# Linear attention and two expert layers: attention rebuilt on strips of the array, half of the weight conversions placed behind it

## The chip, the cores and the metric

The kernel runs on one core of one Trainium2 chip. The metric is device microseconds of one launch; the host's arrangement of arrays before and after the launch is outside it. Before the change three runs gave 2201.4, 2201.72 and 2202.03 us: a median of 2201.72 us.

## The reference

```python
def phi(x):                                     # w_phi: 64 x 128
    proj = einsum('bhsd,df->bhsf', x, w_phi)
    proj = proj - max(abs(proj), axis=-1)
    return concatenate([exp(proj), exp(-proj)])
q_p, k_p = phi(q), phi(k)                       # q, k, v: 4 batches x 8 heads x 576 tokens x 64
kv  = einsum('bhsf,bhsd->bhfd', k_p, v);  z = sum(k_p, axis=2)
x   = (q_p @ kv) / (q_p @ z + 1e-6)             # -> 2304 tokens x 512
h   = x @ w_in;  x = (h * cos(h)) @ w_out       # w_in 512 x 2048, w_out 2048 x 512: 64-bit floats
P   = exp(x @ w_gate - max), 8 rounds of row and column scaling   # 2304 x 8
out = sum over e of P[:, e] * (relu(x @ w1[e]) @ w2[e])           # 8 experts, w1 512 x 1024
```

## The kernel before

Three stages follow each other. **Attention** works on 16 pairs of heads (4 batches x 4 pairs). Of the 576 tokens of a head 512 are "main" and 64 are the "rest"; the rests of two heads fill 128 partitions together. **The first expert layer** goes through blocks 0 to 3 (the main tokens of a batch, 512 columns) and block 4 (all rests, 256 columns, beside block 3) with 16 units of weights, each made of half a unit from `w_in` and half from `w_out`. **The second expert layer** runs over 8 experts x 4 quarters, twice, with a seven-product scheme (`layer1`) and an accumulation (`layer2`).

Products in the expert layers split each operand into a rounded high part (`act_hi`, ScalarE) and the rest (`dve_lo` or `pool_lo`) and add three products (`mm3`). The 64-bit weights of the first layer come as pairs of 32-bit words and are converted on the chip: 32 halves, one for each half unit. For one half (`conversion`, lines 128 to 169) the low word goes through ScalarE (`csgn`), the high word through three VectorE operations (`cmag`: mask, floor with 2^-15, shift) and one that puts sign and low bits together; GpSimd joins them, ScalarE rounds (`csp`), GpSimd makes the rest, and a transfer writes both to device memory (`wd`). `load_unit1` fetches a unit from there (`wsp`, four buffers).

One round of attention works on three pairs at once, each at another stage: the newest pair is loaded, turned (`turn_heads`, transposes of `kraw` and `qraw` into `pa`, split into `Th` and `Tl`) and projected (`project`, a block-diagonal `w_phi` for two heads, three products); the pair before gets its key sums (`key_sums`, `pk`: 2 heads x 2 signs x 5 products, with ones beside `v` for the denominator), its query features (`query_features`, transposes into `pu`) and its quotient (`attend`, `pn`); the oldest is turned back (`emit_x`, `px`). The maximum of the absolute value and the subtraction (`center`, tiles `m` and `u`) are VectorE's, the exponentials (`exps`) ScalarE's. [...]

In attention each engine runs in the written order: while `pinned[0]` is set, every operation is kept in program order. The order of the steps is the string `ORDER`, once a round, 18 rounds in all (line 517). A step `k` resumes the conversion, four times a round, so all 32 halves are through before the first layer begins. Outside attention the planner may bring ready work forward on an engine. In the first layer `moe1_steps` yields four times a unit; for block 0 each second yield resumes whatever is left of the conversion (line 577), and `next_unit` resumes it until the unit asked for is there (line 529). All transfers are issued by SyncE, in one queue.

Of the kernel before, what the change touches and what calls it, by code (L numbers as in the profile page):

```python
# [25 lines left out]
def kernel(ctx: ExitStack, tc: tile.TileContext, q, k, v, w_phi,  # L26
                         moe_w_in, moe_w_out, moe2_w_gate, moe2_w1, moe2_w2, out):
    nc = tc.nc
    B, H, S, D = q.shape
    NT, DM = out.shape  # L30
    DFF = moe_w_out.shape[0]
    NE, _, DF2 = moe2_w1.shape
    P = 128
    NP = H // 2
    KC = DM // P
    NF1 = DFF // P
    NF2 = DF2 // P
    MAIN = 512
    REM = S - MAIN
# [4 lines left out]
    NTT = NT // P  # L44
# [73 lines left out]
    ps_a = actx.enter_context(tc.tile_pool(name="ps_a", bufs=7, space=PSUM, side="right"))  # L118
    turn = [0]

    def apsum(name):
        return ps_a.tile([P, 512], F32, name=name, tag="pa")

    wd = [dpool.tile([P, 2, 2, DM], F32, name=f"wd{f}") for f in range(NF1)]
    win32 = moe_w_in.bitcast(I32)
    wout32 = moe_w_out.bitcast(I32)

    def conversion():
        n = 2 * NF1
        raws, mags, sps = {}, {}, {}  # L130

        def fetch(h):
            f, i = divmod(h, 2)
            raw = vpool.tile([P, DM, 2], I32, name="raw64")
            if i == 0:
                nc.sync.dma_start(out=raw.rearrange("p (k f) t -> p k (f t)", k=KC),
                                  in_=win32[:, f * 2 * P:(f + 1) * 2 * P].rearrange("(k p) f -> p k f", p=P))
            else:
                nc.sync.dma_start(out=raw.rearrange("p f t -> p (f t)"), in_=wout32[f * P:(f + 1) * P, :])
            raws[h] = raw  # L140

        fetch(0)
        yield
        for h in range(n + 1):
            if h > 0:
                sps[h - 1] = vpool.tile([P, 2, DM], F32R, name="csp")
                act_hi(sps[h - 1][:, 0, :], mags[h - 1].bitcast(F32))
            if h < n:
                if h + 1 < n:
                    fetch(h + 1)  # L150
                hw = raws[h][:, :, 1]
                mag = vpool.tile([P, DM], I32, name="cmag", bufs=CB)
                sgn = vpool.tile([P, DM], I32, name="csgn", bufs=CB)
                se.activation(out=sgn.bitcast(F32), in_=raws[h][:, :, 0].bitcast(U32), func=AF.Copy,
                                     scale=2.0 ** -51, bias=2.0)
                ve.tensor_scalar(out=mag, in0=hw, scalar1=2 ** 31 - 1, scalar2=None, op0=ALU.bitwise_and)
                ve.tensor_scalar(out=mag.bitcast(F32), in0=mag.bitcast(F32), scalar1=2.0 ** -15, scalar2=None, op0=ALU.max)
                ve.tensor_scalar(out=mag, in0=mag, scalar1=3, scalar2=None, op0=ALU.logical_shift_left)
                mags[h] = mag
            yield  # L160
            if h < n:
                ve.scalar_tensor_tensor(out=sgn, in0=hw, scalar=-2 ** 31, in1=sgn, op0=ALU.bitwise_and, op1=ALU.bitwise_or)
                ge.tensor_tensor(out=mag, in0=mag, in1=sgn, op=ALU.add)
            if h > 0:
                sp = sps.pop(h - 1)
                pool_lo(sp[:, 1, :], mags.pop(h - 1).bitcast(F32), sp[:, 0, :])
                nc.sync.dma_start(out=wd[(h - 1) // 2][:, (h - 1) % 2, :, :], in_=sp.bitcast(F32))
                done_conv[0] = h // 2
            yield

    vx_t = []
    for i in range(2):
        t = apool.tile([P, 10, P], F32, name=f"vx{i}", bufs=1)
        ge.memset(t, 0.0)
        ge.memset(t[:, 0:8, D:P], 1.0)
        ge.memset(t[0:D, 8, D:P], 1.0)
        ge.memset(t[D:P, 9, D:P], 1.0)
        vx_t.append(t)
# [4 lines left out]
    def load_pair_rest(src, b, p, t):  # L183
        for a in range(2):
            nc.sync.dma_start(out=t[D * a:D * a + D, 8, :], in_=src[b, 2 * p + a, MAIN:S, :])

    def load_pair(src, b, p, nm, part=False):
        t = apool.tile([P, 9, D], F32, name=nm)
        nc.sync.dma_start(
            out=t[:, 0:8, :].rearrange("p (h j) d -> p h (j d)", h=2),  # L190
            in_=src[b, 2 * p:2 * p + 2, 0:MAIN, :].rearrange("h (p j) d -> p h (j d)", j=4))
        if not part:
            load_pair_rest(src, b, p, t)
        return t

    def load_v(b, p):
        t = vx_t[p % 2]
        for a in range(2):
            nc.sync.dma_start(out=t[:, 4 * a:4 * a + 4, 0:D],
                              in_=v[b, 2 * p + a, 0:MAIN, :].rearrange("(p j) d -> p j d", j=4))  # L200
            nc.sync.dma_start(out=t[D * a:D * a + D, 8 + a, 0:D], in_=v[b, 2 * p + a, MAIN:S, :])
        return t

    raw0 = [load_pair(k, 0, 0, "kraw", True)]
    wblk = apool.tile([P, 4, P], F32, name="wblk", tag="u", bufs=4).rearrange("p a f -> p (a f)")[:, 0:2 * P]
    ve.memset(wblk, 0.0)
    nc.sync.dma_start(out=wblk[0:D, 0:P], in_=w_phi)
    nc.sync.dma_start(out=wblk[D:P, P:2 * P], in_=w_phi)
    wblkh = apool.tile([P, 2 * P], F32R, name="wblkh", bufs=1)
    wblkl = apool.tile([P, 2 * P], F32R, name="wblkl", bufs=1)  # L210
    split(wblk, wblkh, wblkl, act_hi, dve_lo)
    wrem = apool.tile([P, P], F32, name="wrem", bufs=1)
    ve.tensor_copy(wrem, wblk[:, P:2 * P])
    load_pair_rest(k, 0, 0, raw0[0])
    raw0.append(load_pair(q, 0, 0, "qraw"))
    GQ = P // KC
    graw = const.tile([P, KC, GQ], F32, name="graw")
    ge.memset(graw, 0.0)
    nc.sync.dma_start(out=graw[:, :, 0:NE], in_=moe2_w_gate.rearrange("(k p) e -> p k e", p=P))
# [15 lines left out]
    def load_heads(b, p):  # L235
        st = {"b": b, "p": p}
        st["raw"] = raw0 if (b, p) == (0, 0) else [load_pair(k, b, p, "kraw"), load_pair(q, b, p, "qraw")]
        st["vx"] = load_v(b, p)
        st["u"], st["kp"], st["qp"], st["T"] = {}, {}, {}, {}
        return st  # L240

    def turn_heads(st, part):
        if part == "r":
            st["Tr"] = apool.tile([P, 2, P], F32, name="Tr", bufs=1)
            pr = apsum("pr")
            for s in range(2):
# [27 lines left out]
    def project_rem(st):  # L274
        pp = apsum("pp")
        for s in range(2):
            pe.matmul(pp[:, s * P:(s + 1) * P], st["Tr"][:, s, :], wrem, start=True, stop=True)
        u = apool.tile([P, 2, P], F32, name="urem", bufs=1)
        center(pp, 2, u)
        st["u"][2] = u[:, 1, :]  # L280
        t = apool.tile([P, 2, P], F32, name="kp1", bufs=1)
        st["kp"][2] = t
        defer(KD, lambda: exps((t[:, 0, :], t[:, 1, :]), u[:, 0, :]))
        yield 0.44

    def project(st, s, unit):
        pp = apsum("pp")
        for w in range(2):
            th, tl = [x[:, 2 * unit + w, :] for x in st["T"][s]]
            mm3(pp[:, 256 * w:256 * w + 256], [((th, tl), (wblkh, wblkl))])  # L290
# [272 lines left out]
    while late:  # L563
        tick()
# [318 lines left out]
```

## Time and profile before

| | before |
|---|---|
| median of three runs | 2201.72 us |
| profiled execution: its own time | 2202.81 us |
| its span, first to last instruction | 2201.0 us |
| mean granted TensorE clock | 0.998 |
| TensorE busy | 2173.4 us (99%), 12871 matmuls |
| VectorE, ScalarE, GpSimd busy | 1311.0, 963.6, 1076.8 us |

The span differs from the execution's own time by what lies around the first and last instruction. Matmuls are pipelined and their ends are modelled: a busy TensorE is one with work under way, not one at its peak. A merged row of the timeline gives the first start and the time to the last end; the spacing of equal instructions is read from it by taking off the length of the last.

### The profile page before, as it was taken

The page shows a single profiled execution, that of the slowest core. Times are in us where ns is not written, and L with a number is a line of the kernel's source. Part 1 is how long each engine was busy: PE and PEld are TensorE (multiplying, and loading weights), DVE is VectorE, ACT ScalarE, POOL GpSimd, SP SyncE. Part 2 cuts the span into 40 slices and gives each one's busy share as a digit, 9 for nine tenths or more (in the row PEclk, how much of TensorE's full clock was granted, in tenths as well). Part 3 has the DMA queues.
Part 4 walks back from the last instruction along what each step waited for, and adds up shares of the span by engine and source line. Part 5 has one row for each costly group of instructions (what it writes and reads, how often), then busy time and mean ns, then how long its engine had stood idle before and what let it go on. Part 6 is the DMA issues. An engine that isn't in the chain of part 4 may idle for free.

```text
span 2201.0 us, 33288 instructions
## 1 busy us (share of the span) xinstructions
PE 2173.4 (99%) x12871; PEld 1940.4 (88%) x12871; DVE 1311.0 (60%) x2492; ACT 963.6 (44%) x1565; POOL 1076.8 (49%) x712
## 2 busy tenths in 40 slices
PE   8999999999999999999999999999999999999999
PEld 8999888887887888988998998998998999999998
DVE  7888744335534876666666655555555555555555
ACT  5666555555553343343343343333433433433431
POOL 2233400000005577577577576576676676676662
PEclk9999999999999999999999999999999999999999
DMA  6766455556433112222222111441111111111101
GB/s 188 242 197 193 141 185 200 195 204 213 139 113 102 39 65 66 86 81 75 77 70 91 60 59 49 139 141 49 40 48 48 46 41 49 49 39 48 49 29 44
DMA packets 143631, 219.57 MB, mean 100 GB/s; under 512 B 36336, under 2 KB 94832, under 8 KB 143472
## 3 DMA queue, kind: packets, MB, share of 16 engines
q1 hardware_dynamic: 143472, 217.44, 30.1%
q8 instruction: 101, 1.65, 0.3%
q14 instruction: 58, 0.48, 0.1%
HBM read 182.93 MB, written 34.47 MB: 99 GB/s over the span
## 4 chain that ended last, share of the span: by engine, by line
PE 84%; DVE 10%; POOL 2%; DMA 1%; issue 1%; SPq 1%; ACT 1%; POOLq 0%; DVEq 0%; ACTq 0%
PE py L70 35%; PE pm L70 31%; PE ph L70 9%; PE acc L70 8%; DVE m L70 2%; DVE u L70 2%; DVE cmag L70 2%; POOL cmag L70 1%; DVE csgn L70 1%; POOL csp L70 1%; DVE rd L70 0%; DVE xn L70 0%; PE pn L70 0%; DMA raw<-in_moe_w_dram 0%; DVE xl L70 0%
## 5 line engine op out<-in xcount | busy, mean ns | idle before, releaser
L787 DVE SCALAR_TENSOR_TENSOR acc<-py,logit,acc 128x512 f32<-128x512 f32 x531 | 396.6, 750 | 322.2 <-PE py L70 322.2
L70 PE MATMUL pm<-xch,w1h 128*128 128x288 f32 x1792 | 531.0, 296 | 3.1 <-DVE t L815 1.3
L70 PE MATMUL pm<-xch,w1l 128*128 128x288 f32 x1792 | 530.6, 297 | 0.0
L70 PE MATMUL pm<-xcl,w1h 128*128 128x288 f32 x1792 | 523.0, 292 | 0.0
L682 POOL TENSOR_TENSOR w1l<-raw,w1h 128x256 fp32r<-128x256 f32 x126 | 97.1, 792 | 824.4 <-ACT w1h L679 824.4
L70 PE MATMUL py<-w2h,hl 128*128 128x512 f32 x1152 | 452.0, 392 | 3.6 <-POOL hl L70 3.6
L70 PE MATMUL py<-w2l,hh 128*128 128x512 f32 x1152 | 451.6, 392 | 0.0
L70 PE MATMUL py<-w2h,hh 128*128 128x512 f32 x1152 | 450.6, 391 | 0.8 <-DVE acc L787 0.8
L70 POOL TENSOR_TENSOR hl<-r,hh 128x1152 fp32r<-128x1152 f32 x128 | 344.7, 2693 | 78.8 <-ACT hh L70 73.0
L70 PEld LDWEIGHTS pm<-xcl,w1h 128*128 128x128 f32 x1792 | 341.1, 190 | 5.3 <-issue 0.4
L70 PEld LDWEIGHTS pm<-xch,w1h 128*128 128x128 f32 x1792 | 336.6, 188 | 9.7 <-DVE t L815 1.6
L70 PEld LDWEIGHTS pm<-xch,w1l 128*128 128x128 f32 x1792 | 336.1, 188 | 0.0
L761 ACT ACTIVATE r<-r 128x1152 f32<-128x1152 f32 x128 | 149.1, 1165 | 268.4 <-DVE r L741 262.1
L70 PEld LDWEIGHTS py<-w2h,hl 128*128 128x128 f32 x1152 | 216.9, 188 | 50.1 <-POOL hl L70 4.3
L70 PEld LDWEIGHTS py<-w2h,hh 128*128 128x128 f32 x1152 | 217.0, 188 | 44.9 <-DVE acc L787 2.8
L70 PEld LDWEIGHTS py<-w2l,hh 128*128 128x128 f32 x1152 | 216.9, 188 | 42.5
L737 ACT COPY keep<-pm 128x288 f32<-128x288 f32 x256 | 101.8, 398 | 343.9 <-PE pm L70 343.8
L741 DVE TENSOR_TENSOR r<-r,pm 128x288 f32<-128x288 f32 x512 | 216.0, 452 | 41.6 <-PE pm L70 41.2
L682 POOL TENSOR_TENSOR w1l<-ssum,w1h 128x1280 fp32r<-128x1280 f32 x63 | 186.7, 2964 | 2.0 <-ACT w1h L679 0.3
L741 DVE TENSOR_TENSOR r<-keep,pm 128x288 f32<-128x288 f32 x128 | 58.2, 455 | 208.3 <-PE pm L70 207.6
L70 PE MATMUL ph<-xh,wsp 128*128 128x512 f32 x512 | 169.5, 392 | 2.7 <-ACT h L70 1.6
L70 PE MATMUL acc<-hh,wsp 128*128 128x512 f32 x512 | 167.2, 389 | 0.6 <-ACT hh L70 0.6
(156 smaller groups left out, 3199.3 us busy)
## 6 DMA issues: line engine op xcount, KB each, us to landing
wsp<-wd SPq DMA_DIRECT2D x128, 512.0 KB, 4.6
raw<-in_moe_w_dram SPq DMA_DIRECT2D x128, 512.0 KB, 3.5
wd<-csp SPq DMA_DIRECT2D x32, 512.0 KB, 3.2
raw<-in_moe_w_in_dram SPq DMA_DIRECT2D x16, 512.0 KB, 4.1
raw<-in_moe_w_out_dram SPq DMA_DIRECT2D x16, 512.0 KB, 4.2
xcd<-xs SPq DMA_DIRECT2D x14, 576.0 KB, 5.2
kraw<-in_k_dram SPq DMA_DIRECT2D x16, 256.0 KB, 4.4
qraw<-in_q_dram SPq DMA_DIRECT2D x16, 256.0 KB, 3.3
```

What stands on the lines that cost most here:

```text
L70: ins = call(*args, **kwargs)
L682: eng.tensor_tensor(out=lo[:, sl], in0=src, in1=hi[:, sl].bitcast(F32), op=ALU.subtract)
L737: nc.scalar.copy(out=t, in_=ps[m])
L741: nc.vector.tensor_tensor(out=r[:, u, th, :], in0=r[:, u, th, :] if a is None else ps[a], in1=ps[b], op=op)
L761: nc.scalar.activation(out=rf, in_=rf, func=AF.Relu)
L787: nc.vector.scalar_tensor_tensor(out=a, in0=py, scalar=pe, in1=a, op0=ALU.mult, op1=ALU.add)
```

## The change

Queries, keys and values reach the kernel already laid out by the host: keys and queries with the head dimension on the partitions, two heads one above the other (64 partitions each), so the transposes and splits of the inputs are gone. The projection is a plain fp32 product of 64 rows for each head, on the upper or the lower half of the array's rows. Key sums and quotients use 64 weight columns at a time, so that their results lie on the lower or upper 64 PSUM partitions, and 66 columns (64 of `v` and two of ones) in place of 128. PSUM in attention is three tiles of two banks (`pa`), one bank for the rests (`sm`) and one (`ph`) for `pk` and `px`; the maximum, the subtraction and the exponentials take eight groups of 128 columns at a time in place of four. A new `ORDER` lists every engine's steps. In each round one half of the first layer's weights is converted, with the floor on GpSimd; halves 0 to 17 start in attention, and `convert` does the rest from the places in block 0 where the generator was resumed before. The inputs of the second layer and the output are laid out in whole rows on the host. The core of the diff:

```diff
-    ps_a = actx.enter_context(tc.tile_pool(name="ps_a", bufs=7, space=PSUM, side="right"))
+    ps_a = actx.enter_context(tc.tile_pool(name="ps_a", bufs=3, space=PSUM, side="right"))
+    ps_r = actx.enter_context(tc.tile_pool(name="ps_r", bufs=1, space=PSUM, side="right"))
...
+    def conv_fetch(h):
+        raw = vpool.tile([P, DM, 2], I32, name="raw64")
+        nc.sync.dma_start(out=raw.rearrange("p f t -> p (f t)"), in_=moe_w32[h // 2, h % 2])
...
+    def conv_floor(h, eng):
+        mag = halves[h]["mag"].bitcast(F32)
+        eng.tensor_scalar(out=mag, in0=mag, scalar1=2.0 ** -15, scalar2=None, op0=ALU.max)
...
+    VW = 66
...
+    def load_heads(b, p):
+        st = {"b": b, "p": p}
+        for nm, src in (("k", k), ("q", q)):
+            st[nm] = apool.tile([P, MAIN], F32, name=f"T{nm}")
+            nc.sync.dma_start(out=st[nm], in_=src[b, p])
+        st["r"] = apool.tile([D, 2, P], F32, name="Tr")
+        nc.sync.dma_start(out=st["r"], in_=qk_rem[b, p])
...
+    def pair_psum(name):
+        return ps_a.tile([P, 2 * MAIN], F32, name=name, tag="pa")
+
+    def project(st, nm):
+        pp = pair_psum("pp")
         for w in range(4):
+            for a in range(2):
+                rows = slice(D * a, D * a + D)
+                pe.matmul(pp[:, MAIN * a + w * P:MAIN * a + (w + 1) * P], st[nm][rows, w * P:(w + 1) * P],
+                          wphi[rows, :], start=True, stop=True)
+        st["p" + nm] = pp.rearrange("p (j f) -> p j f", f=P)
+
+    def project_rest(st):
+        st["small"] = ps_r.tile([P, MAIN], F32, name="sm")
+        for s in range(2):
+            pe.matmul(st["small"][:, s * P:(s + 1) * P], st["r"][:, s, :], wphi[0:D, :], start=True, stop=True)
...
+    def peak(st, nm, n):
+        m = apool.tile([P, 8], F32, name="m", bufs=4)
+        st["m" + nm] = m[:, 0:n]
+        ve.tensor_reduce(out=m[:, 0:n], in_=st["p" + nm], axis=AX.X, op=ALU.max, apply_absolute_value=True)
+
+    def center(st, nm, n):
+        u = apool.tile([P, n, P], F32, name=f"u{nm}", bufs=1 if nm == "k" else 2)
+        ve.tensor_tensor(out=u, in0=st["p" + nm], in1=st["m" + nm].unsqueeze(2).to_broadcast([P, n, P]), op=ALU.subtract)
...
     def key_sums(st):
+        pk = ps_h.tile([P, MAIN], F32, name="pk", tag="ph")
+        kp, kp1, vx = st["kp"], st["kp1"], st["vx"]
         for a in range(2):
             for s in range(2):
+                c = slice((2 * a + s) * VW, (2 * a + s + 1) * VW)
+                for j in range(5):
+                    for h in range(2):
+                        f = slice(D * h, D * h + D)
+                        if j < 4:
+                            pe.matmul(pk[f, c], kp[:, 4 * a + j, s, f], vx[:, 4 * a + j, :], start=(j == 0), stop=False)
+                        else:
+                            pe.matmul(pk[f, c], kp1[:, s, f], vx[:, 8 + a, :], start=False, stop=True)
...
+    def attend(st):
+        pn = pair_psum("pn")
+        kvz, qp, qp1 = st["kvz"], st["qp"], st["qp1"]
+        for a in range(2):
             for j in range(4):
                 for s in range(2):
+                    for h in range(2):
+                        t0 = (4 * a + j) * P + D * h
+                        pe.matmul(pn[D * h:D * h + D, MAIN * a + j * VW:MAIN * a + (j + 1) * VW], qp[:, s, t0:t0 + D],
+                                  kvz[:, 2 * a + s, :], start=(s == 0), stop=(s == 1))
+        for s in range(2):
+            for a in range(2):
+                t = slice(D * a, D * a + D)
+                pe.matmul(pn[t, 4 * VW:5 * VW], qp1[:, s, t], kvz[:, 2 * a + s, :], start=(s == 0), stop=(s == 1))
...
+    def turn_x(st, cur):
...
+        px = ps_h.tile([P, MAIN], F32, name="px", tag="ph")
         for j in range(4):
+            pe.transpose(px[:, j * P:(j + 1) * P], st["xn"][:, j, :, :].rearrange("p a d -> p (a d)"), ident)
+        pz = (cur or {"small": ps_r.tile([P, MAIN], F32, name="sm")})["small"][:, 3 * P:3 * P + D]
+        for a in range(2):
+            t = slice(D * a, D * a + D)
+            pe.matmul(pz[t, :], st["xr"], ident[:, t], start=True, stop=True)
...
+    def convert():
+        h = B * NP + 1
+        conv_round(h)
+        yield
+        conv_rest(h)
+        done_conv[0] = (h + 1) // 2
+        for h in range(h + 1, NHALF):
+            if h + 1 < NHALF and h + 1 not in halves:
+                conv_fetch(h + 1)
+            conv_low(h)
+            conv_size(h)
+            conv_floor(h, ve)
+            conv_high(h)
+            yield
+            conv_join(h)
+            yield
+            conv_round(h)
+            conv_rest(h)
+            done_conv[0] = (h + 1) // 2
+            yield
...
-    ORDER = "t0 c0 k c1 t1 k c2 x c3 k tr f0 f2 p0 L f1 p1 r p2 g0 p3 g2 g1 k"
+    ORDER = "PK F csg PR KS rR d eQ Fr a csp PQ rK sR kvz sK rQ eQr X q c G sQ xh eKr xl n eK p"
...
-    conv = conversion()
+    conv = convert()
     pinned[0] = True
-    for _ in attention():
-        tick()
-    while late:
-        tick()
+    attention()
```

Of the names in `ORDER`, `PK PQ PR` are projections of keys, queries and rests, `F` and `Fr` the transposes of query features, `KS` the key sums, `G` is `attend`, `X` is `turn_x` (all TensorE); `r.` is `peak`, `s.` is `center`, `d` and `c` are conversion, `xl` is the rest of `px`, `n` normalizes (VectorE); `csg csp` (conversion), `eK eKr eQ eQr` (exponentials), `kvz` and `xh` are ScalarE's; `a q p` (floor, rest, join of the conversion) are GpSimd's.

## Rows read from the trace of the kernel before

**Rows 1.** Busy time by stretch: length, then PE, PEld, DVE, ACT, POOL, clock, DMA.
```profile
28.18:248.60 220.42, 217.44 (x1828) 206.75 (x1827) 185.49 (x427) 135.80 (x306) 70.38 (x56) 1.00 0.66 202
263.90:356.50 92.60, 90.81 (x400) 73.83 (x400) 38.76 (x59) 49.01 (x86) 8.00 (x7) 1.00 0.57 195
```

**Rows 2.** The page's chain that ended last, by engine.
```profile
PE 84%; DVE 10%; POOL 2%; DMA 1%; issue 1%; SPq 1%; ACT 1%; POOLq 0%; DVEq 0%; ACTq 0%
```

**Rows 3.** Timeline of VectorE, one round apart: start us, length us, instruction.
```profile
99.54 0.68 DVE L70 TENSOR_TENSOR xl<-px,xh 128x512 fp32r<-128x512 f32 x1
...
115.49 0.68 DVE L70 TENSOR_TENSOR xl<-px,xh 128x512 fp32r<-128x512 f32 x1
```

**Rows 4.** Timeline of TensorE, one round.
```profile
104.84 3.07 PE L70 MATMUL pn<-kvz,qp 128*64 128x128 f32 x24
...
108.19 2.40 PE L70 MATMUL pk<-vx,kp 128*128 128x128 f32 x20
...
114.61 0.36 PE L70 MATMUL pp<-wblkh,Th 128*128 128x256 f32 x1
114.81 0.28 PE L70 MATMUL pp<-wblkl,Th 128*128 128x256 f32 x1
114.93 0.28 PE L70 MATMUL pp<-wblkh,Tl 128*128 128x256 f32 x1
```

**Rows 5.** The gate and `pick`: timeline of TensorE, then the gate's stretch.
```profile
356.50 1.07 PE L70 MATMUL ph<-x2f,graw 128*32 128x512 f32 x8
...
359.25 0.95 PE L70 MATMUL ph<-pick,lt 128*128 128x8 f32 x8
...
356.54:356.56 0.02, 0.02 (x4) 0.02 (x8) 0.00 (x0) 1.00 0.53 205
```

**Rows 6.** Groups of VectorE by shape, 60 to 250 us: busy, mean ns.
```profile
L70 DVE TENSOR_REDUCE m<-pp 128x4 f32<-128x512 f32 x48 | 32.7, 681 | 0.0
L70 DVE TENSOR_TENSOR u<-pp,m 128x512 f32<-128x512 f32 x47 | 32.5, 692 | 1.6
...
L70 DVE SCALAR_TENSOR_TENSOR csgn<-raw,csgn 128x512 int32<-128x512 int32 x24 | 16.4, 682 | 0.0
...
L70 DVE TENSOR_SCALAR cmag<-raw 128x512 int32<-128x512 int32 x24 | 10.1, 423 | 21.7 <-POOL csp L70 19.9 <-DMA vx<-in_v_dram 1.8
...
L70 DVE TENSOR_TENSOR urem<-pp,m 128x256 f32<-128x256 f32 x12 | 5.1, 424 | 0.4
L70 DVE TENSOR_REDUCE m<-pp 128x2 f32<-128x256 f32 x12 | 5.0, 415 | 0.0
```

**Rows 7.** Groups of ScalarE and GpSimd by shape.
```profile
L70 ACT ACTIVATE kp<-u 128x512 f32<-128x512 f32 x48 | 27.6, 623 | 8.0 <-DVE u L70 8.0
...
L70 ACT ACTIVATE kp<-urem 128x128 f32<-128x128 f32 x24 | 5.9, 293 | 0.0
...
L70 POOL TENSOR_TENSOR csp<-cmag,csp 128x512 fp32r<-128x512 f32 x32 | 40.9, 1280 | 0.0
```

**Rows 8.** Start of the kernel: timeline of TensorE, and a stretch by engine.
```profile
10.31 0.41 PE L70 MATMUL pp<-wblkl,Th 128*128 128x256 f32 x1
10.52 0.41 PE L70 MATMUL pp<-wblkh,Tl 128*128 128x256 f32 x1
...
8.00:10.00 2.00, 2.00 (x11) 2.00 (x10) 1.00 (x2) 0.84 (x2) 0.00 (x0) 1.00 0.51 99
```

**Rows 9.** Transfers by line: count, KB each, us to landing.
```profile
wsp<-wd SPq DMA_DIRECT2D x128, 512.0 KB, 4.6
...
wd<-csp SPq DMA_DIRECT2D x32, 512.0 KB, 3.2
...
raw<-in_moe_w_out_dram SPq DMA_DIRECT2D x16, 512.0 KB, 4.2
```

**Rows 10.** Timelines of GpSimd and of SyncE's queue.
```profile
270.73 1.74 POOL L671 TENSOR_TENSOR ssum<-raw 128x512 f32<-128x512 f32 x1
...
43.99 1.06 SPq L101 DMA_DIRECT2D wsp<-wd  x2
```

More of the change, by code (lines that the diff above doesn't have):

```diff
@@ L43 @@
     T0 = [sum(TILES[:i]) for i in range(NBLK)]
-    NTT = NT // P
     NPASS = 2
@@ L126 @@
[L126 to L169, printed above, removed]
@@ new lines, in conv_join, with conv_round, conv_rest @@
+    def conv_join(h):
+        st = halves[h]
+        ge.tensor_tensor(out=st["mag"], in0=st["mag"], in1=st["sgn"], op=ALU.add)
+    def conv_round(h):
+        st = halves[h]
+        st["sp"] = vpool.tile([P, 2, DM], F32R, name="csp")
+        act_hi(st["sp"][:, 0, :], st["mag"].bitcast(F32))
+    def conv_rest(h):
+        st = halves.pop(h)
+        pool_lo(st["sp"][:, 1, :], st["mag"].bitcast(F32), st["sp"][:, 0, :])
+        nc.sync.dma_start(out=wd[h // 2][:, h % 2, :, :], in_=st["sp"].bitcast(F32))
@@ L196, in load_v @@
[L196 to L215, printed above, removed]
+    def load_heads(b, p):
[5 more added lines that the diff above has]
+        nc.sync.dma_start(out=st["r"], in_=qk_rem[b, p])
+        return st
@@ L272, in exps @@
         se.activation(out=out[1], in_=src, func=AF.Exp, scale=-1.0)
[L274 to L290, printed above, removed]
[L291 to L299 removed]
+    def key_features(st):
+        t = apool.tile([P, 8, 2, P], F32, name="kp")
+        st["kp"] = t
+        exps((t[:, :, 0, :], t[:, :, 1, :]), st["uk"])
@@ L326, in attend @@
-    def attend(st, unit):
-        pn = apsum("pn")
-        kvz, qp = st["kvz"], st["qp"][unit]
-        if "xn" not in st:
-            st["xn"] = apool.tile([P, 5, 2, D], F32, name="xn", bufs=XB)
-        if unit == 2:
-            for a in range(2):
-                for s in range(2):
-                    pe.matmul(pn[0:D, a * P:(a + 1) * P], qp[:, s, a * D:(a + 1) * D], kvz[:, a, s, :],
-                                     start=(s == 0), stop=(s == 1))
-            pv = pn[0:D, 0:2 * P].rearrange("p (a c) -> p a c", a=2)
-            xo = st["xn"][0:D, 4, :, :]
-            n, pr = 2, D
-        else:
+                c = slice((2 * a + s) * VW, (2 * a + s + 1) * VW)
@@ new lines, in turn_queries, with turn_rest, query_features, query_features_rest @@
+    def turn_queries(st):
+        pu = pair_psum("pu")
+        for j in range(8):
+            pe.transpose(pu[:, j * P:(j + 1) * P], st["uq"][:, j, :], ident)
+        st["pu"] = pu
+    def turn_rest(st, cur):
+        st["pv"] = cur["small"][:, 2 * P:3 * P]
+        pe.transpose(st["pv"], st["ur"][:, 1, :], ident)
+    def query_features(st):
+        t = apool.tile([P, 2, 8 * P], F32, name="qp", bufs=1)
+        exps((t[:, 0, :], t[:, 1, :]), st["pu"])
+        st["qp"] = t
+    def query_features_rest(st):
+        t = apool.tile([P, 2, P], F32, name="qp1", bufs=1)
+        exps((t[:, 0, :], t[:, 1, :]), st["pv"])
+        st["qp1"] = t
@@ L402 @@
+    STEP1 = {"F": turn_queries, "Fr": turn_rest, "KS": key_sums, "kvz": keep_sums, "eQ": query_features,
+             "eQr": query_features_rest, "G": attend, "n": normalize}
     hps = [ps_h]
```

323 lines of the change are left out of this document (156 added, 167 removed).

## The prediction

> **What bounds the kernel now.** I began with the busy time of each engine by stage. Attention (the stretch from 28 to 249 us) and block 0 of the first expert layer (264 to 356 us) both have TensorE busy for 98% or more, and VectorE is busy for 84% of attention and 42% of block 0 [rows 1]. The page's chain of the whole span gives TensorE 84% and VectorE 10% [rows 2]. Neither says which engine limits attention, since the end of a matmul is modelled; so I read one round of its loop. The split of `px` (`xl<-px`) starts at 99.54 and again at 115.49 us: a pair of heads takes 15.95 us [rows 3]. In the timeline of TensorE inside such a round, 20 passes of 128 columns in `pk` take 2.40 us, the last of them 0.27, so one starts every (2.40 - 0.27) / 19 = 0.112 us [rows 4]. A round issues 132 such instructions (40 `pk`, 40 `pn`, 24 `pp` with the rounded operands and 4 with `wrem`, 24 transposes counted one each: 8 `pa`, 2 `pr`, 9 `pu`, 4 `px`, 1 `pz`): 132 x 0.112 = 14.8 us, and the rest of the 15.95 us is mostly changes of operand type or tile shape: 8 narrow and 16 full `pn` together take 3.07 us, where 24 x 0.112 + 0.16 would be 2.85 [rows 4]. TensorE bounds attention. VectorE, at 84% of 15.95 us = 13.4 us a round, is the next limit.
>
> **The change, part by part.** The second expert layer and blocks 1 to 4 of the first keep their instructions; what is left is the round of attention (16 rounds of full work), its start, and the conversions moved behind it.
>
> TensorE, by `project`, `key_sums`, `attend`, `turn_queries`, `turn_x`. A matmul of fp32 data is two instructions (the 20 `pk` products of the code are 40 in a round), a transpose one. After: `PK` and `PQ` 8 products each of 64 rows and 128 columns, `PR` 2: 36 instructions. `key_sums` 40 products, `attend` 36 and two in `turn_x`, 66 or 64 columns each, with 64 weight columns: 156 instructions. Transposes 8 + 1 + 4 = 13. A pass of 66 columns lasts 66/128 x 0.112 = 0.058 us. Taken one after another, this is 156 x 0.058 + 36 x 0.112 + 13 x 0.112 = 9.0 + 4.0 + 1.5 = 14.5 us, and 9 changes of tile shape at 0.17 (between the 0.08 that the first `pp` after `pu` takes longer than the next, 0.20 to 0.12 from start to start, and the 0.22 of the `pn` row [rows 4]) add 1.5: 16.0 us, what a round takes now. So the whole question is whether two halves of the array work at once.
>
> For column strips the trace answers. The gate's 8 instructions of 512 columns, four strips of 32, take 1.07 us together [rows 5]. One after another, at 512/128 x 0.112 = 0.45 each, they would take 3.6. At 356.54 us four matmuls and eight weight loads are under way at once. So loads and passes in separate strips run side by side: the 156 cost 156 x 0.029 = 4.5 us. For row halves (`PK`, `PQ`, in two PSUM banks) no row exists: 4.0 us if they take turns, 2.0 if not. I take 2.0, since the column strips are the nearest row. Sum 4.5 + 2.0 + 1.5 + 1.5 = 9.5 us.
>
> [...]
>
> VectorE. The trace has no operation on 1024 columns; from 256 to 512 a reduction goes from 415 to 681 ns and a subtraction from 424 to 692 [rows 6], so 1024 should be 681 + 2 x 266 = 1.21 and 692 + 2 x 268 = 1.23 us. Round: `rK rQ` 2.4, `sK sQ` 2.5, `rR sR` 0.8, conversion 0.42 + 0.42 + 0.68 = 1.5 (one half, the floor is on GpSimd) [rows 6], `xl` 0.9 with its small part [rows 3], `normalize` about 1.4 (one product of 512 at 0.69, four small ones taken at 0.18): 9.5 us by durations. In the round before, the 17 groups from which rows 6 are cut add up to 14.6 us against 13.4 busy, since neighbours overlap; at that ratio 8.7, so 8.7 to 9.5. What falls away is the split `Tl` (two of 512), one of two conversions (about 2.0) and the fixed part of the halved operations.
>
> ScalarE: from 293 ns at 128 columns to 623 at 512 [rows 7] an exponential of 1024 takes 1.06; four of these, four small, two of the conversion, `kvz`, `xh`: under 8 us, hidden. GpSimd: a floor, a join and a rest at 1.28 or less [rows 7]: 3.8 us, hidden. The floor on GpSimd (`a`) has no row; between 0.5 and 2 us it is covered, because `c` waits for it only behind `rK sR sK rQ`, 4 us of VectorE.
>
> Waits in the round. `PR` and `key_sums` use single banks and wait for `xl` of the round before; behind them on TensorE stand `Fr PQ X G`. `F` waits for `sQ` of the round before, `PQ` for `normalize`, through three two-bank tiles. From `PR`, VectorE does `rR d rK sR sK` in 3.7 us while TensorE does `key_sums`, `Fr`, `PQ` in 3.9; `rQ c sQ` (3.4) stand beside `X`, `G` and the next `PK` (4.3). The two fit with little to spare, so I add 0.6 us to the 9.5: a round of 10.1 us. Bounds: 8.7 (VectorE alone), 16.0 (no overlap), and the rivals below.
>
> 16 rounds x (15.95 - 10.1) = 93.6 us gained. Start: the first keys still have to land, and the first `key_sums` comes after a projection, 3.7 us of VectorE and two exponentials; TensorE's passes are at half rate until 11.4 us now (0.41 us and a spacing of 0.21 for a pass that later takes 0.28 and 0.12), though the granted clock reads 1.00 there [rows 4, 8]. I count nothing, +-3 us.
>
> Block 0. Halves 18 to 31 are converted beside it: VectorE 14 x 2.0 = 28 us, ScalarE 18, GpSimd 36, of 92.6 us in which VectorE is busy 39, ScalarE 49, GpSimd 8 [rows 1]: covered. Transfers: 0.57 of 92.6 us carry 195 GB/s now, 342 GB/s at a full share. 14 halves read and written are 14.7 MB, 43 us more beside the 53: 96 of 92.6 us, so about 4 us may show. Lower end 0: TensorE has no slack to give back there. Upper end: in the written order halves 26 to 31 are asked for only when units 13 to 15 are loaded, and such a half needs fetch 4.2, about 5.5 us on engines, write 3.2, read 4.6 [rows 9]: 17.5 us, less the 5.4 us of matmuls for one unit, three times: 36 us. Against it stands that ready work is brought forward: GpSimd works at 270.73 us on weights of the second layer, which the program asks for after the last block [rows 10], and `wsp` loads begin at 43.99. I take 4.
>
> The host lays out inputs and output in whole rows: fewer pieces per transfer, all behind a busy TensorE; the last stores differ by +-1 us. I count nothing.
>
> Sum, against the profiled execution (span 2201.0, own time 2202.8): 2202.8 - 93.6 + 4 = 2113.2. The median of the runs shown is 1.1 us lower: 2112 us.
>
> **The rivals.**
> (1) A floor on the rate of small matmuls, the case that ends on the other side. Place: TensorE's instruction stream in `PK PQ key_sums attend`, 192 matmuls with 192 loads a round. If one can start only every f us, the round is 192 f + 3.0; it is slower than 15.95 from f = 0.068. For it: no stretch of the trace sustains a pair of load and matmul in less than 0.10 us (8 `pick` passes of 8 columns in 0.95 [rows 5]), and at 0.10 the round is 22.2 us, +100 +4: 2306 us. Against it: `pick` loads 128 weight columns, which by itself may take that long, and the gate starts four matmuls and eight loads within 0.06 us.
> [...]
> (2) Halves that take turns, the change not doing what it says. Round 16.0: 2206 us. Rows 5 speak against it for columns. For rows alone it costs 2.0 us a round: 2144.
> (3) Block 0 waits for its late conversions: +36 in place of +4, 2144 us.
> [...]
>
> **How the numbers follow.** The forecast, with its own range of 2092 (round 8.8) to 2150 (rows in turns, or a round of 12): 0.66. A weaker floor or part of the overlap, 2150 to 2195: 0.13. Late conversions: 0.08. No overlap: 0.04. Floor above 0.068: 0.06. Clock: 0.03. Of the case without overlap half counts as slower and half as within 0.2% (some 4.4 us, about what a measurement can tell from no change): slower 0.11, within it 0.02, faster 0.87. The range of 2092 to 2190 leaves out about 0.16.
>
> **What would show it.** Right: the split of `px` comes round every 9 to 11 us; `key_sums` (80 instructions) takes about 2.4 us and `attend` 2.1, `PK` 0.9 to 1.0; the first layer starts near 170 us; VectorE is busy for some 90% of attention. Wrong: `key_sums` near 4.6 us (turns) or above 5.4 (floor 0.068 and more); TensorE idle in block 0 waiting for `wsp`; passes of 128 columns at 0.21 us spacing. The step I trust least is the rate of 192 small loads and matmuls in a row.

## The result

The changed kernel takes 2141.07 us (median of 4 runs, 2140.14 to 2144.19) against 2201.88 us (4 runs) on the same chip: a ratio of 0.9724, 95% interval [0.9708, 0.9741]. The forecast was 2112 us, its range 2092 to 2190: the time lies 29 us above the one and inside the other. The profiled execution has a span of 2140.1 us. Two marks in TensorE's timeline divide the 60.9 us gained on the span of before. The end of the last `pn`, where attention ends, moved from 264.1 to 169.7 us: 94.4 us earlier (forecast 93.6). From there to the first instruction of the gate, which closes block 0 of the first expert layer, it was 92.4 us and is 128.6 us: 36.1 us later (forecast 4). What follows is 2.6 us shorter, as it is in every kernel below (0.6 to 2.8 us). So attention gave what was forecast, and block 0 gave back more than a third of it.

### The profile after

By stretch (columns as in [rows 1]), attention and then block 0 of the changed kernel:

```profile
20.00:163.00 143.00, 139.95 (x3009) 125.63 (x3004) 125.25 (x230) 99.53 (x190) 58.90 (x45) 1.00 0.75 222
169.70:298.20 128.50, 105.52 (x404) 81.01 (x404) 77.42 (x116) 64.53 (x115) 47.97 (x37) 0.89 0.73 253
```

TensorE is busy for 98% of attention and VectorE for 88%. In block 0, TensorE's 404 matmuls now take 105.52 of 128.50 us; its granted clock was 1.00 there before [rows 1] and is 0.89. The page's chain that ended last does not show what happened in block 0, since it sums over the whole span: TensorE has 89% of it and VectorE 3%, where they had 84% and 10% [rows 2].

```profile
PE 89%; DVE 3%; issue 3%; POOL 2%; ACT 1%; DMA 1%; SPq 0%; POOLq 0%; DVEq 0%
```

VectorE's timeline (start, length) has the split of `px`, 15.95 us apart in [rows 3], every 9.6 us:

```profile
35.66 0.68 DVE L68 TENSOR_TENSOR xl<-px,xh 128x512 fp32r<-128x512 f32 x1
45.23 0.68 DVE L68 TENSOR_TENSOR xl<-px,xh 128x512 fp32r<-128x512 f32 x1
...
152.81 0.69 DVE L68 TENSOR_TENSOR xl<-px,xh 128x512 fp32r<-128x512 f32 x1
162.38 0.68 DVE L68 TENSOR_TENSOR xl<-px,xh 128x512 fp32r<-128x512 f32 x1
```

A round in TensorE's timeline, against [rows 4]:

```profile
37.06 0.71 PE L68 MATMUL sm<-wphi,Tr 64*128 64x128 f32 x4
37.70 2.56 PE L68 MATMUL pk<-vx,kp 128*64 128x66 f32 x80
40.19 0.33 PE L68 MATMUL sm<-ident,ur 128*128 128x128 f32 x1
40.45 1.16 PE L68 MATMUL pp<-wphi,Tq 64*128 64x128 f32 x16
41.54 0.66 PE L68 MATMUL px<-ident,xn 128*128 128x128 f32 x4
42.12 0.34 PE L68 MATMUL sm<-ident,xr 128*64 128x64 f32 x4
42.29 2.28 PE L68 MATMUL pn<-kvz,qp 128*64 128x66 f32 x72
44.50 1.16 PE L68 MATMUL pp<-wphi,Tk 64*128 64x128 f32 x16
45.59 1.09 PE L68 MATMUL pu<-ident,uq 128*128 128x128 f32 x8
46.62 0.71 PE L68 MATMUL sm<-wphi,Tr 64*128 64x128 f32 x4
```

From one `sm<-wphi` to the next it is 9.56 us, with no idle time between. The 80 instructions of `pk` start every (2.56 - 0.22) / 79 = 0.030 us, and the 16 of a projection every (1.16 - 0.28) / 15 = 0.059 us, where one pass of 128 columns at a time started every 0.112 [rows 4].

The groups by shape on VectorE, ScalarE and GpSimd in attention, against [rows 6, 7], confirm the sizes that had been extrapolated (1.21, 1.23 and 1.06 us, and a floor on GpSimd between 0.5 and 2):

```profile
L68 DVE TENSOR_REDUCE m<-pp 128x8 f32<-128x1024 f32 x29 | 35.3, 1217 | 0.0
L68 ACT ACTIVATE kp<-uk 128x1024 f32<-128x1024 f32 x30 | 30.0, 1056 | 0.3 <-DVE uk L68 0.3
L68 POOL TENSOR_SCALAR cmag<-cmag 128x512 f32<-128x512 f32 x15 | 22.3, 1486 | 43.6 <-DVE cmag L68 41.0 <-DMA raw<-in_moe_w_dram 2.7
L68 DVE TENSOR_TENSOR uq<-pp,m 128x1024 f32<-128x1024 f32 x15 | 18.3, 1217 | 0.0
```

Block 0 is where the loss lies. TensorE's groups there name what the idle time ahead of them waited for:

```profile
L68 PE MATMUL ph<-xh,wsp 128*128 128x512 f32 x136 | 50.4, 437 | 10.6 <-DMA wsp<-wd 5.8 <-ACT h L68 2.5 <-DVE xl L68 2.2
L68 PE MATMUL acc<-hh,wsp 128*128 128x512 f32 x128 | 44.2, 416 | 10.3 <-ACT hh L68 10.3
```

Of its 23 us without a matmul it waits 10.3 for the rounded hidden layer (`hh`) and 5.8 for weights of the coming unit (`wsp`). The longest of these waits in the timeline of all engines (start, length, engine; in brackets the idle time before and its releaser):

```profile
269.65 2.72 SPq L99 DMA_DIRECT2D wsp<-wd  x2
269.68 1.26 POOL L68 TENSOR_TENSOR cmag<-cmag,csgn 128x512 int32<-128x512 int32 x1 [0.96 <-DVE cmag L68]
269.91 1.58 DVE L68 SCALAR_TENSOR_TENSOR y<-t,y 128x512 f32<-128x512 f32 x1 [0.30 <-ACT t L68]
...
271.67 1.27 POOL L68 TENSOR_TENSOR csp<-cmag,csp 128x512 fp32r<-128x512 f32 x1 [0.73 <-ACT csp L68]
272.19 1.30 DVE L68 TENSOR_TENSOR h<-y,h 128x512 f32<-128x512 f32 x1 [0.70 <-ACT y L68]
272.97 0.32 SPq L162 DMA_DIRECT2D wd<-csp  x1
273.52 0.62 ACT L68 CAST hh<-h 128x512 fp32r<-128x512 f32 x1 [1.37 <-DVE h L68]
...
274.19 0.80 PE L68 MATMUL acc<-hh,wsp 128*128 128x512 f32 x1 [5.96 <-ACT hh L68]
```

Two things can be read there. First, `y` and `h`, which take 0.69 us at 282.44 and 283.83 us, with GpSimd idle, take 1.58 and 1.30 here, and each ends about 0.6 us after a GpSimd operation that had begun before it (270.94 and 271.49 us, 272.94 and 273.49). VectorE seems to wait for the end of GpSimd's operation and only then to run; the trace doesn't show why. Experiment 8 tests what this costs. Second, the weights of the coming unit are asked for only at 269.65 us, so TensorE has no other matmuls to put into the gap. The matmuls that end the gap last 0.80 us, where the last one before it (267.85 us) took 0.39: the granted clock in the stretches around the gap is 1.00 until 272 us and 0.50 from 274 us on (columns as above):

```profile
270.00:272.00 2.00, 0.00 (x0) 0.00 (x0) 1.49 (x1) 1.02 (x2) 1.27 (x2) 1.00 0.97 293
272.00:274.00 2.00, 0.00 (x0) 0.00 (x0) 1.30 (x1) 0.63 (x2) 0.94 (x1) 0.56 1.00 397
274.00:276.00 2.00, 1.81 (x4) 1.18 (x5) 1.79 (x4) 0.72 (x2) 0.00 (x0) 0.50 0.98 307
```

### The profile page after: what moved, and what is told of

It is laid out like the page before. It is cut to its first block, busy times and chain, and to the rows that moved or that the text cites. A ratio compares the mean times of both kernels' runs of the same rounds, so it can differ in the third digit from the quotient of the medians.

```text
span 2140.1 us, 35117 instructions
## 1 busy us (share of the span) xinstructions
PE 2089.5 (98%) x14039; PEld 1846.2 (86%) x14039; DVE 1274.5 (60%) x2311; ACT 934.0 (44%) x1452; POOL 1104.3 (52%) x729
## 4 chain that ended last, share of the span: by engine, by line
PE 89%; DVE 3%; issue 3%; POOL 2%; ACT 1%; DMA 1%; SPq 0%; POOLq 0%; DVEq 0%
PE py L68 36%; PE pm L68 32%; PE ph L68 8%; PE acc L68 7%; PE pk L68 2%; PE pp L68 1%; PE pn L68 1%; POOL cmag L68 1%; PE sm L68 1%; PE pu L68 1%; POOL csp L68 1%; PE px L68 0%; ACT csp L68 0%; DVE logit L818 0%; DVE r L748 0%
## 5 line engine op out<-in xcount | busy, mean ns | idle before, releaser
L68 PE MATMUL ph<-xh,wsp 128*128 128x512 f32 x512 | 174.7, 403 | 11.0 <-DMA wsp<-wd 5.8
L68 PE MATMUL acc<-hh,wsp 128*128 128x512 f32 x512 | 169.6, 396 | 10.3 <-ACT hh L68 10.3
```

Of the source, the lines that this page charges most:

```text
L68: ins = call(*args, **kwargs)
```

## The experiments

All are edits of the changed kernel. The prediction's theory was that the late conversions of halves 18 to 31 are covered in block 0. Since block 0 lost 36 us, the theories to tell apart are: the order in which the conversions are written and resumed; the transfers; and the arithmetic, by VectorE's time, or by VectorE and GpSimd blocking each other. "Stretch" is from the end of the last `pn` to the first gate instruction in the profiled execution: 92.4 us before, 128.6 after. It is read from one execution of each kernel, whose time lies up to 3.7 us from the median.

**1. No late conversions.** Units 9 to 15 use the weights of units 0 to 6; halves 18 to 31 aren't converted.

```
-        for h in range(h + 1, NHALF):
+        for h in range(h + 1, h + 1):
...
-        units.append(load_unit1(len(units) % NF1))
+        units.append(load_unit1(len(units) % NF1 % 9))
```

> Leaves out the conversion of halves 18 to 31 and gives units 9 to 15 the weights of units 0 to 6, so all loads of block 0 stay. Theory A (the late conversions, asked for in the written order, are what block 0 gives back): from the last pn to the first gate matmul 92 to 95 us, as before the change, in place of 128.5, and a time of 2105 to 2110 us. Rival B (the junction: ph waits for px and xl, a clock at half rate after it): at most 12 of the 36 us go, 2129 us or more. Rival C (transfers: 14 halves read and written beside 16 units) also expects 2105 to 2110, since the transfers go with the conversions; the next run tells A from C.

Measured: 2110.25 us (2106.58 to 2113.56), ratio to before 0.9583 [0.9569, 0.9597]; stretch 95.8 us. Block 0 by engine:

```profile
167.00:262.60 95.60, 91.77 (x404) 74.47 (x404) 39.26 (x60) 49.55 (x87) 9.20 (x9) 1.00 0.54 185
```

The late conversions cost 32.8 of the 36.1 us by the stretches, 30.8 us by the medians; the other 3.3 us of the stretch stay unexplained. Without the 4 us of block 0 the forecast is 2108 us, and this kernel takes 2110. The same 404 matmuls take 91.77 us here and 105.52 in the changed kernel. So 13.7 of the 32.8 us are matmuls that last longer (`ph` 393 ns here, 437 there) and 19.1 are idle time.

**2. Conversion resumed at three of four places** instead of two.

```
-            if blk == 0 and i % 2:
+            if blk == 0 and i % 4:
```

> Only the places change at which the late conversion is resumed in block 0: three of four in place of two of four, so that a half is written for every unit from the start and none is forced at units 13 to 15; the same work and the same bytes. Theory A: the burst at 250 to 280 us and its waits go, 15 to 28 us of the 36, time 2113 to 2126. Rival C (block 0 is bound by its 31 MB of transfers, 94 us at the 336 GB/s that a full share gives): 6 us or less, 2135 to 2141.

Measured: 2137.14 us (2135.92 to 2139.46), 0.9707 [0.9692, 0.9721]; stretch 123.7. The written order, which the prediction's third rival blamed, is worth 4 us by the medians and 5 by the stretch, far from the 15 to 28 that theory A expected.

**3. All halves converted in attention**, two in a round.

```
...
-    ORDER = "PK F csg PR KS rR d eQ Fr a csp PQ rK sR kvz sK rQ eQr X q c G sQ xh eKr xl n eK p"
+    ORDER = "PK F csg PR KS rR c2 d eQ Fr a p2 csp PQ rK sR kvz sK rQ eQr X q csp2 d2 c G sQ csg2 q2 xh eKr xl a2 n eK p"
...
```

> All 32 halves are converted in the new attention, two a round, with both floors on GpSimd; nothing is left for block 0. By the busy times of the round (VectorE 8.8 + 1.5, GpSimd 4.0 + 4.0, ScalarE 6.9 + 1.2, TensorE 9.7 with its waits) VectorE sets a round of 10.6 to 11.4 us, +14 to +27 us in attention, block 0 back to 92 to 95 us (-34): 2121 to 2135 us. If the conversions hide beside TensorE (round below 10.2): 2107 to 2115. If the chain through GpSimd stalls VectorE and ScalarE in order (round above 12): 2145 or more, and placing half of them later was needed.

Measured: 2152.24 us (2148.92 to 2156.82), 0.9775 [0.9758, 0.9791]; `pn` ends 45.6 us later and the stretch is 93.4. Attention from 40 to 200 us by engine, and two groups of VectorE in it:

```profile
40.00:200.00 160.00, 129.46 (x2577) 115.50 (x2573) 142.55 (x243) 94.52 (x184) 99.53 (x76) 0.95 0.78 242
```

```profile
L68 DVE TENSOR_SCALAR cmag<-raw 128x512 int32<-128x512 int32 x25 | 22.6, 906 | 15.6 <-DMA raw<-in_moe_w_dram 11.4 <-POOL csp L68 4.2
L68 DVE SCALAR_TENSOR_TENSOR csgn<-raw,csgn 128x512 int32<-128x512 int32 x25 | 22.0, 882 | 0.0
```

TensorE is down to 129.46 of 160 us. VectorE is busy for 142.55 and waits another 15.6 for raw words and for GpSimd, so nothing of its time is left; beside a second half on GpSimd its own conversion operations lengthen from 418 to 906 and from 686 to 882 ns. How much of the longer round is the lengthening and how much the waits, the run doesn't separate. Moving 14 halves out of block 0 gains 35 us there and costs 46 in attention: of these two places the change's is the cheaper one.

**4. Key sums with whole columns**: one matmul of 128 weight columns in place of two strips of 64, the same products.

```
-                        if j < 4:
-                            pe.matmul(pk[f, c], kp[:, 4 * a + j, s, f], vx[:, 4 * a + j, :], start=(j == 0), stop=False)
+                    if j < 4:
+                        pe.matmul(pk[:, c], kp[:, 4 * a + j, s, :], vx[:, 4 * a + j, :], start=(j == 0), stop=False)
...
```

> The key sums alone go back to 128 weight columns (40 instructions of 66 columns in place of 80 on two strips). If the strips run side by side and a load of 128 columns sets the pace (0.10 to 0.112 us): KS 4.1 to 4.6 us in place of 2.56, round 11.2 to 11.8, 24 to 33 us more, 2165 to 2174. If the strips take turns: KS stays near 2.6 us and the time near 2141. If VectorE bounds the round (8.8 of 9.7 us busy): about 10 us more at most.

Measured: 2175.65 us (2 runs, 2173.34 and 2177.97), 0.988 [0.9861, 0.99], just above the 2165 to 2174 expected; `pn` ends 34.9 us later. TensorE's timeline:

```profile
105.11 4.68 PE L68 MATMUL pk<-vx,kp 128*128 128x66 f32 x40
...
116.64 4.68 PE L68 MATMUL pk<-vx,kp 128*128 128x66 f32 x40
```

The round is 11.53 us. 40 instructions take 4.68 us where 80 of half the width take 2.56. One whole-column instruction starts every (4.68 - 0.28) / 39 = 0.113 us, as long as with 128 moving columns (0.112 [rows 4]): what sets that pace is not the 66 columns. The strips of 64 weight columns are the source of the gain in `pk`. How much of it is the smaller weight load and how much two strips at work at once, the run doesn't separate.

**5. Row halves in turns**: all matmuls of a projection on one half of the rows, then all on the other.

```
-        for w in range(4):
-            for a in range(2):
+        for a in range(2):
+            for w in range(4):
```

> The projections do all products of the upper row half first, then those of the lower, in place of alternating. If row halves run side by side only for neighbours in the stream: PK and PQ 1.9 to 2.1 us in place of 1.16, round 11.2 to 11.6, 25 to 30 us more. If the order does not matter: PK 1.2 us, the time unchanged.

One run: 2152.66 us; `pn` ends 14.0 us later. A projection in TensorE's timeline:

```profile
107.45 1.71 PE L68 MATMUL pp<-wphi,Tq 64*128 64x128 f32 x16
```

1.71 us against 1.16, two in a round: 1.1 us of a round of 10.65. Halves that alternate overlap (0.059 us each); halves in turns do so much less (0.095, where a pass of 128 columns over all rows started every 0.112 [rows 4]). The time, 11.6 us more, lies between the two expectations.

**6. Late arithmetic alone, and late transfers alone.** The first fetches no half after half 19, stores none of the late ones, and lets units 9 to 15 load the weights of units 0 to 6. The second fetches the halves and stores the raw words, without arithmetic.

```
 # arithmetic alone
...
-                conv_fetch(h + 1)
+                halves[h + 1] = {"raw": halves[h]["raw"]}
...
 # transfers alone
...
-            conv_low(h)
-            conv_size(h)
...
-            conv_rest(h)
+            nc.sync.dma_start(out=wd[h // 2].bitcast(I32)[:, h % 2, :, :].rearrange("p s f -> p (s f)"),
+                              in_=halves.pop(h)["raw"].rearrange("p f t -> p (f t)"))
...
```

> The arithmetic of the late halves alone: halves 19 to 31 work on the words of half 18, none of them is fetched or stored, and units 9 to 15 load the weights of units 0 to 6. Resumption as in the changed kernel. Theory A (arithmetic in order on VectorE, ScalarE and GpSimd holds up the evacuations of block 0): 2130 to 2141 us, ScalarE still idle before csp for some 30 us. Rival C (transfers, and the store and loads in one queue): 2108 to 2116 us.

> The transfers of the late halves alone: each is fetched and its raw words are stored in place of the two parts, 14.7 MB as before, with no arithmetic; units 9 to 15 load the weights of units 0 to 6. Rival C in its plain form (the bytes fill the 16 engines): 94 us for block 0 at 336 GB/s, 2112 to 2120 us, and more only if the mix runs slower than 336. If what counts is neither arithmetic nor bytes alone but the chain fetch, arithmetic, store, load through one in-order queue: both this run and the one without transfers stay below 2120.

Measured: arithmetic 2137.39 us (2137.0 to 2140.58), 0.9711 [0.9695, 0.9727], stretch 123.3; transfers 2122.32 us (2119.53 to 2122.67), 0.9636 [0.9621, 0.965], stretch 106.8. Block 0 by engine, arithmetic first:

```profile
170.80:294.00 123.20, 103.80 (x404) 81.59 (x404) 87.82 (x116) 64.73 (x115) 50.42 (x37) 0.90 0.44 153
```

```profile
170.30:277.00 106.70, 95.77 (x404) 74.91 (x404) 39.98 (x60) 49.50 (x87) 10.19 (x9) 0.98 0.87 297
```

Of 32.8 us the arithmetic by itself costs 27.5 and the transfers by themselves 11.0; they overlap in part. In the first TensorE waits for no DMA, but 7.5 us for `hl` and 5.9 for `hh`. VectorE's operations lengthen there without the late transfers (`hl` 1.77, 1.75 and 1.76 us at 203.88, 215.77 and 225.15 us, 0.71 in block 0 of before), and hardly beside the transfers without arithmetic (60 operations busy for 39.98 us, 39.26 in experiment 1): it is not the transfers that hold VectorE up. In the second a load of `wsp` lands 6.4 us after its issue (4.6 in [rows 9]). With 0.87 of the DMA time used the transfers come within 14 us of filling the stretch.

**7. Late stores from GpSimd's queue**, with three of four places.

```
-        nc.sync.dma_start(out=wd[h // 2][:, h % 2, :, :], in_=st["sp"].bitcast(F32))
+        (nc.sync if h < B * NP + 1 else nc.gpsimd).dma_start(out=wd[h // 2][:, h % 2, :, :], in_=st["sp"].bitcast(F32))
```

> As the run with three of four places, and the stores of the late halves are issued from GpSimd's own queue, behind the operation that they wait for, so that SyncE's queue holds only loads. If the store's wait at the head of SyncE's queue (75 us in that run) delays the fetches and unit loads: 8 to 20 us less than its 2137, 2117 to 2129. If the bytes or the arithmetic bind: 2134 to 2140. [...]

Measured: 2136.03 us (2133.7 to 2140.22), 0.9703 [0.9688, 0.9717], against 2137.14 in 2, with a stretch of 121.2 us for 123.7: a wait in SyncE's queue isn't what costs the 30 us.

**8. GpSimd out of block 0**: join and rest of the late halves on VectorE; and the join alone. The edit begins at half 17, whose end falls behind attention too, so that it moves 15 joins and 15 rests.

```
-        ge.tensor_tensor(out=st["mag"], in0=st["mag"], in1=st["sgn"], op=ALU.add)
+        (ge if h < B * NP + 1 else ve).tensor_tensor(out=st["mag"], in0=st["mag"], in1=st["sgn"], op=ALU.add)
...
 # only in the first of the two
-        pool_lo(st["sp"][:, 1, :], st["mag"].bitcast(F32), st["sp"][:, 0, :])
+        (pool_lo if h < B * NP + 1 else dve_lo)(st["sp"][:, 1, :], st["mag"].bitcast(F32), st["sp"][:, 0, :])
```

> Join and rest of the late halves (18 to 31) go from GpSimd to VectorE; nothing else is changed, so GpSimd has only the 7 us of the layer's own work beside block 0. Theory D: the 27 us that the late arithmetic costs come from VectorE and GpSimd lengthening each other's SBUF operations (cmag 1.5 us in place of 0.42, the hidden layer's split hl 1.76 in place of 0.69) and from ScalarE, whose rounding of a half waits in order for GpSimd's join (33 us in 15 waits). With both gone cmag is back at 0.42, hl at 0.70, and TensorE's waits for hl and hh shrink to some 3 us; what is left of the 36 us is the transfers' 12 and a few: stretch from the last pn to the gate 105 to 113 us, time 2115 to 2126. Rival: VectorE is simply short of time. It then has 39 us of its own work and 14 halves of 0.42 + 0.42 + 0.68 + 0.69 + 0.69 = 2.9 us, 80 of some 105 us, in bursts that stand ahead of xl and hl: the stretch stays at 125 to 130 us and the time at 2137 to 2145.

> Only the join of the late halves (18 to 31) goes from GpSimd to VectorE, the rest stays on GpSimd (14 operations in block 0 in place of 28). Theory D, with the waiting of ScalarE as its main part: the join is what ScalarE's rounding waits for, so the 33 us of waits vanish and most of the 27 us with them: time 2118 to 2128, near that of the kernel with both moved. Theory D, with the lengthening as its main part: half of the GpSimd operations still run beside VectorE's, half of the gain: 2128 to 2134. Rival (VectorE short of time): 2137 or more.

Measured: both moved 2128.19 us (2124.81 to 2128.82), 0.9662 [0.9647, 0.9676], stretch 112.3; the join alone 2134.39 us (2131.94 to 2136.15), 0.9693 [0.9677, 0.9709], stretch 120.1. Block 0 by engine with both moved:

```profile
169.00:281.20 112.20, 97.87 (x404) 76.78 (x404) 81.38 (x146) 65.31 (x115) 7.54 (x7) 0.95 0.84 289
```

Two groups of VectorE from 175 us on, of the changed kernel (to 298 us) and then of this one (to 290 us, which takes in the start of the next block):

```profile
L68 DVE TENSOR_TENSOR h<-y,h 128x512 f32<-128x512 f32 x16 | 15.1, 950 | 9.2 <-ACT y L68 9.0
...
L68 DVE TENSOR_SCALAR cmag<-raw 128x512 int32<-128x512 int32 x13 | 7.3, 565 | 1.6 <-DMA raw<-in_moe_w_dram 1.6
```

```profile
L68 DVE TENSOR_TENSOR h<-y,h 128x512 f32<-128x512 f32 x18 | 12.4, 687 | 3.7 <-ACT y L68 3.7
...
L68 DVE TENSOR_SCALAR cmag<-raw 128x512 int32<-128x512 int32 x13 | 5.5, 421 | 1.9 <-DMA raw<-in_moe_w_dram 1.9
```

VectorE executes 30 operations more (146 for 116), is busy 4 us longer, and block 0 is 16.3 us shorter: `h` goes from 950 to 687 ns, `cmag` from 565 to 421. That VectorE was short of time falls; that its operations last longer beside GpSimd's stands, though the gain ends a little short of the 2115 to 2126 us expected. By the medians it is 12.9 us, and 6.7 with the join alone.

ScalarE's rounding waits for the join (total us, times, longest): for GpSimd's in the changed kernel, for VectorE's with the join alone moved and with both.

```profile
ACT csp L68 <- POOL cmag L68: 33.0, 15, 4.2
...
ACT csp L68 <- DVE cmag L68: 13.8, 9, 2.9
...
ACT csp L68 <- DVE cmag L68: 13.7, 12, 2.9
```

With the join alone moved the stretch is 8.5 us shorter, about half of 16.3, as half of GpSimd's late operations are. The other 7.8 us come without a change in that wait, and `h` goes from 950 to 802 and then to 687 ns. This speaks for the lengthening as the larger part. But the moved operations are also shorter on VectorE (0.71 and 0.73 us for 1.28 and 1.27 on GpSimd in attention), and the median of the join alone lies 0.4 us above the 2128 to 2134 expected for the lengthening, so the shares aren't settled.

**9. The same with three of four places, and with the stores moved too**: the edits of 8, 2 and 7 together.

```
-            if blk == 0 and i % 2:
+            if blk == 0 and i % 4:
...
 # only in the second
-        nc.sync.dma_start(out=wd[h // 2][:, h % 2, :, :], in_=st["sp"].bitcast(F32))
+        (nc.sync if h < B * NP + 1 else nc.gpsimd).dma_start(out=wd[h // 2][:, h % 2, :, :], in_=st["sp"].bitcast(F32))
```

> Join and rest of the late halves on VectorE, as in the kernel without GpSimd, and the conversion is resumed at three of four places in block 0 instead of two. That kernel took 112.3 us from the last pn to the gate, 16.5 more than without late conversions; transfers alone account for 11. Theory F: the other 5 are bursts, halves written together just before the units that need them, standing on VectorE and ScalarE ahead of hh and hl (VectorE busy 18.4 of 20 us at 240 to 260, TensorE waiting 13 us for hh). Spread out, the stretch falls to 105 to 109 us and the time to 2120 to 2125. Rival: the transfers at 0.85 of the DMA time set the rest, whatever the order: 111 to 114 us, 2127 to 2131.

> The same, and the stores of the late halves are issued from GpSimd's queue, on which nothing else waits in block 0, so that a store that waits for its half no longer stands ahead of wsp loads on SyncE's queue. If the order of that queue costs something, 3 us or more are gained on the kernel with three of four: stretch 102 to 106, time 2116 to 2122. If the rate of the transfers is what is left: within 2 us of it. With GpSimd at work the same move had gained 2.4 us in the stretch.

Measured: 2127.84 us (5 runs, 2126.31 to 2129.28), 0.9665 [0.9652, 0.9678], stretch 113.7; and 2126.47 us (4 runs, 2125.22 to 2130.58), 0.9663 [0.965, 0.9676], stretch 110.2. Block 0 by engine, of each:

```profile
169.90:283.50 113.60, 98.89 (x404) 75.91 (x404) 80.73 (x146) 65.11 (x115) 7.65 (x7) 0.97 0.83 282
```

```profile
169.60:279.70 110.10, 96.88 (x404) 76.23 (x404) 79.69 (x146) 64.30 (x115) 16.41 (x22) 0.97 0.84 295
```

Neither differs from 2128.19 us. The bursts were no cost of their own: with GpSimd out of the stretch the order is worth nothing that these runs can tell. Of the 16.5 us that remain above experiment 1, the transfers by themselves account for 11.0; that the rest is theirs too is argued from the DMA share and not shown. All three of these kernels beat both the kernel before and the changed one; which of them is fastest can't be told.

## Why the prediction was wrong in one step and right in the others

**TensorE's round: right.** Forecast 9.5 us of TensorE and a round of 10.1; measured 9.56. The terms, by the starts of the stages: strips 2.49 (`pk`) + 2.21 (`pn`) + 0.17 (`xr`) = 4.9 us for 4.5; row halves 2 x 1.09 + 0.64 = 2.8 for 2.0; transposes 1.03 + 0.26 + 0.58 = 1.9 for 1.5; the changes of shape, 1.5 in the sum, are inside these. Experiments 4 and 5 show what strips and alternating halves are worth by taking them away. Only the reason behind one price fell: a pass of 66 columns with whole weights is not 0.058 us but 0.113, so the 0.029 of the sum is not half of a pass that is shorter by its columns. The 0.6 us added for VectorE wasn't needed: it is 88% busy, and TensorE has no gap in the round shown.

**The start: off, and hidden by the round.** It had been counted at nothing within 3 us. The first split of `px` starts at 35.7 us in both kernels, so the first of 16 rounds gained nothing; the 15 intervals from it to the last split gained 93.2 us, 6.2 each, where 5.85 was forecast. The errors, 5.9 us lost in the first round and 5.4 gained in the others, cancel: that the sum came within 1 us is luck. Three rounds are longer than the rest (10.33, 9.78 and 10.99 us); where TensorE pauses in them (0.60 us before 61.80, 1.16 before 103.74) the profile shows nothing that it waits for, and why stays open.

**Block 0: the step that failed,** "VectorE 14 x 2.0 = 28 us, ScalarE 18, GpSimd 36, of 92.6 us in which VectorE is busy 39, ScalarE 49, GpSimd 8 [rows 1]: covered". Its term was 4 us and measured 36.1, of which the late conversions are 32.8. The amounts were close, except VectorE's. VectorE's own work and the conversions' were put at 39 + 28 us, GpSimd's at 8 + 36, the DMA time at 96 us; the rows after give 77.4, 48.0 and 0.73 x 128.5 = 94. None of these fills 128 us. Wrong was the conclusion from amounts to cover. It assumed that VectorE's 28 us run as if GpSimd's 36 were not beside them, whereas both lengthen beside each other: VectorE 77.4 - 39.3 = 38 us in place of 28, GpSimd's join 1.48 us for 1.28 in attention. The chain from `ph` to `hh`, operations on ScalarE and VectorE in turns, then outlasts what TensorE has ready, and behind the longest gap the clock is low (0.50 there, 0.89 over the stretch). For transfers it assumed that 96 us in 92.6 would show as the difference, while the engines' share doesn't get beyond 0.87 over a stretch in any of these runs: 11.0 us by themselves, not 4. One of the prediction's own signs of being wrong came up here, TensorE idle in block 0 for `wsp`, 5.8 us. That the time still lies in the range is luck: its upper part had been kept for a weaker floor or less overlap in attention.

**The third rival** had the size (2144 us) and a chance of 0.08, but another mechanism: halves 26 to 31 asked for too late, 12 us three times. Experiment 2 gives that order 4 to 5 us, and 9 gives it nothing once GpSimd is out. The floor on small matmuls (0.068 us or more), the halves that take turns and a lower clock in attention didn't occur: 80 matmuls with their loads, one every 0.030 us (`pk`), experiments 4 and 5, and a granted clock of 1.00.

How much of the longer matmuls is the clock isn't settled: at a clock of 0.89 they take 13.7 us more than in experiment 1, at 0.94 they take 13.6 more in experiment 2 and 7.9 in 7.

## What to carry to other kernels

Busy times that add up to less than the stretch don't show that work is hidden: ask of each pair of engines whether they hold each other up, and what the bounding engine has ready while its inputs come late. Price an operation moved beside a busy neighbour on the neighbour too; here 14 halves that looked free cost 31 to 33 us, and taking one engine out of the stretch, at more work for the other, got 13 to 16 of them back. And an idle gap on TensorE can cost more than its length: behind the gap of 5.96 us the granted clock was 0.50 and the first matmuls took 0.80 us for 0.39.

## What was not expected of the hardware

- VectorE operations beside a GpSimd operation: `y` 1.58 and `h` 1.30 us for 0.69, ending about 0.6 us after GpSimd's operation does.
- Matmuls on alternating row halves start every 0.059 us and in turns every 0.095; 64-column strips start every 0.030 us and whole columns every 0.113, for the same 66 moving columns.
- With no matmul from 268.2 us, the granted clock was 1.00 until 272 and 0.50 from 274; after that the first matmuls of 512 columns took 0.80 us (0.39 at a granted clock of 1.00).
